# Attention and two MLPs: the second product of the second MLP's first group as seven block products, and stages for x's parts in dead columns of x

## The chip, the cores and the metric

The kernel runs on one core of one Trainium2 chip. The metric is device time in microseconds (us) of one execution, as the median of the runs. TensorE (PE) multiplies, VectorE (DVE) and ScalarE (ACT) work element by element, SyncE (SP) issues the DMAs. Each engine takes its instructions in the order in which they stand in its queue.

## What is computed

A linear attention gives x (2304 tokens, 512 features), and two MLPs follow it. Both have the same shapes; they differ in the function between their two products.

```python
kv = np.einsum('bhsd,bhse->bhde', k, v)
out = np.einsum('bhsd,bhde->bhse', q, kv)
rms = np.sqrt(np.mean(out * out, axis=-1, keepdims=True) + 1e-06)
x = (out / rms * g_norm)            # brought to [2304, 512]
h = x @ w_in                        # [512, 2048], first MLP
x = (np.maximum(h, 0.0) + np.log1p(np.exp(-np.abs(h)))) @ w_out
h = x @ w_in2                       # second MLP
y = np.maximum(0.01 * h, h) @ w_out2
```

All of it is float32. On PE every factor is held as a high part in fp32r and a remainder ("parts"), and each float32 product is three matmuls: high by high, high by low, low by high.

## The kernel before

**Tiling.** The 2304 tokens are cut into NTP = 3 pairs of blocks of BN = 384 tokens. Each MLP's hidden features are cut into NG = 4 groups of 512, so the two MLPs have groups 0 to 3 and 4 to 7. A step t is one group with one token pair, t = 3 * group + pair; there are 24 steps, 0 to 23. Group 4, the second MLP's first group, is steps 12 to 14.

**First product of a step** (`product`, L845). The products of x and the first weight are done as seven block products instead of eight (a scheme of Strassen's kind): 2 stages of 7 products of 6 matmuls with 384 columns, 84 matmuls in a step. The seven combinations of x's blocks ("x's parts") are in `xe`; they are worked out once for each MLP and token pair (`x_part`, with `split_part`), stored to DRAM (`part_store`), and loaded again for each group (`x_load`). In the steps just ahead of the second MLP (t = 11, 12, 13) the parts of the next pair are made from the first MLP's result, which lies in `xy`: four combinations, whose parts go through two stages in `rc` (`xstage`, 6 KiB each), and three plain blocks, split directly into `xe`. A stage can be written again when the store that reads it has landed.

**Second product.** It lags: while step t's first products run, step t - 1's second products run between them. In the groups named in `SG` it is also seven block products (`second`, its `piece`): in the first MLP with 84 matmuls of 384 columns (L1101), in the second with 126 matmuls of 256 columns (L1096) in a step. For that DVE makes differences of the activations (`g_part`, L976), ACT and DVE split seven blocks of them (`parts`, L874 and L879), and both work out seven combinations of the second weight (`w2_part`, L1027 and L1030). Each block's result is added to `xy` by DVE (`to_y`, L1074). In the other groups, 0, 3 and 4, it is the plain product (`quarter`): L1196 in groups 0 and 3, and in group 4 L1214, 72 matmuls of 512 columns in a step, whose results are copied to `xy` (`to_xy`, L729 by DVE or L730 by ACT), since group 4 is the first to write there.

**Buffers.** `xy` holds x and, in place, each MLP's result. `rb` holds the activations' parts and the second weight's (`w2s` of the plain products, `wS` of the block products, in two layouts: one for groups 1 and 2, one for groups 5 to 7). `rc`, `mf` and `lf` hold raw and decoded weights and activations; `cS` is the ring of activation blocks of the block products.

**Order.** All operations are recorded as `op(cost by engine, function, reads, writes)`, and `Plan.run` puts them in order: it walks through a modelled time and takes on each engine, of the operations that are ready, the one due first. The products on PE keep the order in which they are written. The order on DVE, ACT and SP follows from costs and due times.

Of the kernel before, what the change touches and what calls it, by code (L numbers as in the profile page):

```python
# [133 lines left out]
def linear_attention_two_mlps(  # L134
# [209 lines left out]
    def t_d(n, fast=False):  # L344
        return 0.08 + n * (0.8e-3 if fast else 1.04e-3)
# [431 lines left out]
    def x_part(tp, i, stages=(), B=None):  # L777
# [218 lines left out]
    def w2_part(g, i):  # L996


        def blk(a, u):
            at = (3 + 4 * u) * KI // 4  # L1000
            ap = bufs["rc"][:, at:at + 2 * DM].rearrange("p (m f) -> p m f", m=2)
            return ap[:, :, a * 256:(a + 1) * 256]

        def bk(a, u):
            return [k_ for m in range(2) for k_ in fS[u][m].keys(1024 * a, 1024 * (a + 1))]
# [19 lines left out]
        w_ = wS[g // NG][PROD[i][2]]  # L1025
# [25 lines left out]
    def second(t):  # L1051
# [8 lines left out]
        def to_y(i, bank, j0, j1):  # L1060
# [11 lines left out]
            xk = xyk(kcs, c0, n // len(kcs))  # L1072
            op(
                {"D": t_d(n)}, lambda e: nc.vector.tensor_tensor(dst, src, dst, ALU.add),  # L1074
                xk, [("ps", bank)] + xk,
            )

        def piece(i, j):
            w_ = wS[g // NG][PROD[i][2]]
# [224 lines left out]
    for s in range(2 * NT2 + 2):  # L1304
# [17 lines left out]
        for i in range(7):  # L1322
            if t == 0 and i in (0, 3):
                plain(s, i // 3)
            if t < NT2:
# [7 lines left out]
                if t + 1 in fresh and t + 1 > NTP and u == 0:  # L1333
                    x_part((t + 1) % NTP, i, xstage)
# [25 lines left out]
        if g + 1 < 2 * NG:  # L1360
# [14 lines left out]
            if g and not by_pairs and no >= 4:  # L1375
                w2_decode(g + 1, no - 4)
# [36 lines left out]
```

## Time and profile before

| | us |
|---|---|
| median of 3 runs | 800.98 (800.06 to 803.91) |
| the profiled execution | 801.74 |
| its span, first to last instruction | 800.0 |
| PE busy | 787.8 |
| DVE busy | 644.2 |
| ACT busy | 505.9 |

The profiled execution is 0.1% above the median. Busy time is the union of an engine's instructions in the trace, so two that overlap count once; PE is busy without a break from about 85 us to the end. The steps are seen in the trace by their 84 matmuls of L845: step 12 starts at 417.45 us, step 13 at 448.65, step 14 at 480.54, step 15 at 511.92, step 16 at 543.29, step 18 at 602.46. Since the second product lags by a step, group 4's plain second product lies in steps 13 to 15.

### The profile page before, as it was taken

Reading aid. Unit: us, or ns where it says so; the run is one execution under the profiler, and the core shown is the slowest. Engines: PE = TensorE matmul, PEld = TensorE weight load, DVE = VectorE, ACT = ScalarE, POOL = GpSimd, SP = SyncE. Lnnn points to the kernel's source line nnn. Section 1 sums busy time; section 2 is a strip of 40 time slices with the busy share of each in tenths; the row PEclk is TensorE's granted clock in tenths of the full one; section 3 lists DMA queues with packets and bytes.
Section 4 is the critical chain, followed back from the end, with each engine's and each line's share of the span. In section 5 each row is a group of like instructions: output and inputs, shape, how many; then the busy total and the mean of one; then the engine's idle time right before and its main releaser. Section 6 shows DMA issues by size and latency. Waiting matters only on the chain.

```text
span 800.0 us, 12956 instructions
## 1 busy us (share of the span) xinstructions
PE 787.8 (98%) x4962; PEld 774.4 (97%) x4962; DVE 644.2 (81%) x1046; ACT 505.9 (63%) x832; POOL 19.0 (2%) x35
## 2 busy tenths in 40 slices
PE   7899999999999999999999999999999999999997
PEld 6899999999999999999999988989999999999997
DVE  6897996978899987983688866748789997996776
ACT  5788986777666675584476676748457654554341
POOL 3310000000000000000000000000000000000000
PEclk9999999999999999999999999999999999999999
DMA  9990992875864783585776986866745763653814
GB/s 305 320 348 2 344 392 100 325 247 234 319 218 174 291 315 128 217 319 194 289 289 227 401 304 246 313 210 222 275 166 198 295 235 120 252 195 122 315 40 120
DMA packets 77294, 192.48 MB, mean 241 GB/s; under 512 B 11568, under 2 KB 50480, under 8 KB 77232
## 3 DMA queue, kind: packets, MB, share of 16 engines
q1 hardware_dynamic: 75344, 190.73, 66.0%
q10 hardware_dynamic: 1888, 0.92, 0.4%
q8 instruction: 39, 0.64, 0.3%
q14 instruction: 23, 0.19, 0.1%
HBM read 152.31 MB, written 39.32 MB: 240 GB/s over the span
## 4 chain that ended last, share of the span: by engine, by line
PE 95%; DVE 2%; ACT 1%; DMA 1%; SPq 1%; issue 0%; ACTq 0%; DVEq 0%
PE ps L845 42%; PE ps L1096 17%; PE ps L1196 12%; PE ps L1101 11%; PE ps L1214 6%; PE ps L461 2%; PE ps L424 1%; PE ps L939 1%; PE ps L545 1%; DMA mf<-in_moe_w_in_dram 1%; PE ps L416 1%; PE ps L467 0%; SPq L384 0%; PE ps L427 0%; DVE ra L701 0%
## 5 line engine op out<-in xcount | busy, mean ns | idle before, releaser
L845 PE MATMUL ps<-ra 128*128 128x384 f32 x1932 | 387.7, 335 | 0.0
L845 PEld LDWEIGHTS ps<-ra 128*128 128x128 f32 x1932 | 334.9, 188 | 3.8
L874 ACT ACTIVATE rb<-mf 128x768 fp32r<-128x768 f32 x131 | 110.8, 846 | 84.0 <-PE ps L1096 39.2
L1096 PE MATMUL ps<-rb 128*128 128x256 f32 x1134 | 153.1, 281 | 0.0
L1096 PEld LDWEIGHTS ps<-rb 128*128 128x128 f32 x1134 | 148.7, 189 | 0.0
L879 DVE TENSOR_TENSOR rb<-mf,rb 128x768 fp32r<-128x768 f32 x131 | 124.9, 954 | 24.2 <-ACT rb L874 23.5
L1074 DVE TENSOR_TENSOR xy<-ps,xy 128x512 f32<-128x512 f32 (+2 forms) x213 | 116.2, 549 | 30.7 <-PE ps L1096 20.1
L1196 PE MATMUL ps<-rb 128*128 128x384 f32 x576 | 113.7, 334 | 0.0
L1150 DVE TENSOR_TENSOR mf<-ps,mf 128x384 f32<-128x384 f32 x118 | 65.3, 554 | 54.2 <-PE ps L845 53.3
L1196 PEld LDWEIGHTS ps<-rb 128*128 128x128 f32 x576 | 101.1, 188 | 0.0
L1101 PE MATMUL ps<-rb 128*128 128x384 f32 x504 | 100.9, 334 | 0.0
L1143 ACT ACTIVATE mf<-ps 128x384 f32<-128x384 f32 x118 | 57.7, 490 | 58.2 <-PE ps L845 55.1
L1101 PEld LDWEIGHTS ps<-rb 128*128 128x128 f32 x504 | 88.6, 188 | 0.0
L1214 PE MATMUL ps<-rb 128*128 128x512 f32 x216 | 56.8, 394 | 0.0
L1214 PEld LDWEIGHTS ps<-rb 128*128 128x128 f32 x216 | 39.9, 188 | 5.7
L860 ACT ACTIVATE mf<-mf 128x768 f32<-128x768 f32 (+1 forms) x44 | 29.8, 678 | 16.6 <-DVE mf L1150 16.5
L866 ACT ACTIVATE mf<-mf 128x384 f32<-128x384 f32 (+1 forms) x42 | 27.6, 657 | 18.9 <-DVE mf L1150 18.8
L976 DVE TENSOR_TENSOR mf<-mf 128x768 f32<-128x768 f32 x40 | 38.1, 952 | 0.9 <-ACT mf L866 0.3
L1027 ACT ACTIVATE rb<-rc 128x512 fp32r<-128x512 f32 x35 | 21.8, 626 | 6.9 <-PE ps L1214 2.4
L1030 DVE TENSOR_TENSOR rb<-rc,rb 128x512 fp32r<-128x512 f32 x35 | 23.9, 684 | 1.1 <-ACT rb L1027 1.1
L730 ACT ACTIVATE xy<-ps 128x384 f32<-128x384 f32 (+1 forms) x32 | 17.3, 541 | 11.0 <-PE ps L1196 8.9
L461 PE MATMUL ps<-kvm,qt 128*128 128x128 f32 x128 | 18.8, 295 | 2.0 <-DVE xn L523 1.5
(120 smaller groups left out, 791.1 us busy)
## 6 DMA issues: line engine op xcount, KB each, us to landing
ra<-xscr SPq DMA_DIRECT2D x131, 768.0 KB, 6.2
xscr<-ra SPq DMA_DIRECT2D x30, 768.0 KB, 6.9
mf<-in_moe_w_in_dram SPq DMA_DIRECT2D x18, 512.0 KB, 6.6
xscr<-rc SPq DMA_DIRECT2D x12, 768.0 KB, 3.8
mf<-in_moe_w_out_dram SPq DMA_DIRECT2D x17, 512.0 KB, 5.8
lf<-in_moe_w_out_dram SPq DMA_DIRECT2D x15, 512.0 KB, 4.0
lf<-in_moe_w_in_dram SPq DMA_DIRECT2D x14, 512.0 KB, 7.4
qa<-in_q_dram SPq DMA_DIRECT2D x16, 256.0 KB, 5.2
```

The costliest lines, as they stand in the source:

```text
L461: nc.tensor.matmul(ps[4 + i][:, r * P:(r + 1) * P], qt[i][:, at_[r]:at_[r] + P], kvm[i], start=True, stop=True,)
L845: nc.tensor.matmul(o, w_[:, a, c:c + P], e_[:, b, kk, :], start=(not on and kk == 0 and n == 0), stop=(kk == 1 and n == 2), skip_group_che ...
L874: {"A": t_a(n)}, lambda e: nc.scalar.activation(g[:, 0, :, :], c.ap, AF.Copy),
L879: lambda e: nc.vector.tensor_tensor(g[:, 1, :, :], c.ap, g[:, 0, :, :].bitcast(F32), ALU.subtract),
L976: lambda e: nc.vector.tensor_tensor(to.ap, x.ap, y.ap, ALU.subtract),
L1074: {"D": t_d(n)}, lambda e: nc.vector.tensor_tensor(dst, src, dst, ALU.add),
L1096: nc.tensor.matmul(y[:, 256 * (j % 2):256 * (j % 2 + 1)], G_[:, a, m, js], w_[:, b, m, :], **flags)
L1101: nc.tensor.matmul(y[:, :BN], w_[:, a, m, js], G_[:, b, m, :], **flags)
L1143: {"A": t_a(BN)}, lambda e: nc.scalar.activation(c[:, m, :], src, AF.Copy),
L1150: lambda e: nc.vector.tensor_tensor(c[:, m, :], src, c[:, m, :], ALU.add),
L1196: nc.tensor.matmul(y[:, :BN], w_[m][:, a, js], G_[:, b, m, :], start=(u == 0 and m == 0 and i == 0), stop=(u == 1 and m == 1 and i == 2),)
L1214: nc.tensor.matmul(y, G_[:, a, m, js], w_[m][:, b, :], start=(u == 0 and m == 0 and i == 0), stop=(u == 1 and m == 1 and i == 2),)
```

## The change

Group 4 enters `SG`: its second product becomes seven block products of 256 columns, as in groups 5 to 7. What that needs is moved:

- `wS` has one layout for all groups.
- Group 4's second weight is decoded into `half` (in `lf` and `mf`) in the last two stages of group 3, and `w2_part` takes it from there, with `sqr` for its temporary block.
- The results of the first four blocks that meet a column of `xy` are copied (by DVE or ACT), those of the other three added.
- The temporaries of x's combinations for pairs 1 and 2 are in `rc` (`xt_late`), where the stages were; the stages for these two pairs are columns of `xy` (`Dead`): those of the pair before, whose x parts have all been taken and whose second result isn't written yet. Such a stage is four rows of 384 elements in a partition instead of one run of 1536.

```diff
+    xt_late = [Reg("rc", at * KI, [2, BN]) for at in (3, 6)]
+
+    class Dead:
+        def __init__(self, c):
+            self.c = c
+        def __getitem__(self, i):
+            return xy[:, :, self.c:self.c + BN].bitcast(F32R).rearrange(
+                "p (a b) n -> p a b n", a=2
+            )[i]
...
-    SG = (1, 2, NG + 1, NG + 2, NG + 3)
+    SG = (1, 2, NG, NG + 1, NG + 2, NG + 3)
...
-    wS = [
-        {j: Reg("rb", at * KI, [2, 2, 256]) for j, at in zip((1, 4, 5, 6, 3, 2, 0), ats)}
-        for ats in ((46, 50, 30, 34, 38, 42, 26), (38, 42, 46, 50, 30, 34, 26))
-    ]
+    wS = {
+        j: Reg("rb", at * KI, [2, 2, 256])
+        for j, at in zip((1, 4, 5, 6, 3, 2, 0), (46, 50, 30, 34, 38, 42, 26))
+    }
...
+        x_ = xt_late if stages and tp else xt
...
     def part_store(tp, i, e_):
+        def fn(e):
+            if isinstance(e_, Dead):
+                nc.sync.dma_start(
+                    out=xscr[7 * tp + i].rearrange("p (k n) -> p k n", k=KC),
+                    in_=xy[:, :, e_.c:e_.c + BN],
+                )
+            else:
+                nc.sync.dma_start(out=xscr[7 * tp + i], in_=flat(e_).ap.bitcast(F32))
...
     def w2_part(g, i):
+        f_ = half[::-1] if g == NG else fS
...
-        r.append((lambda: fT.ap, fT.keys()))
+        r.append(
+            (lambda: sqr.bitcast(F32).rearrange("p (m f) -> p m f", m=2), [("sqr", 0), ("sqr", 1)])
+            if g == NG else (lambda: fT.ap, fT.keys())
+        )
...
-            op(
-                {"D": t_d(n)}, lambda e: nc.vector.tensor_tensor(dst, src, dst, ALU.add),
-                xk, [("ps", bank)] + xk,
-            )
+            to_xy(dst, src, n, g == NG and i in (0, 1, 2, 6), bank, xyk(kcs, c0, n // len(kcs)))
...
-                    x_part((t + 1) % NTP, i, xstage)
+                    tp = (t + 1) % NTP
+                    x_part(tp, i, [Dead((2 * tp - 2 + j) * BN) for j in range(2)] if tp else xstage)
...
-            if g and not by_pairs and no >= 4:
+            if g == NG - 1 and no >= 4:
+                decode_pair(F + 2 * (no - 4), 1, 5 - no)
+            elif g and not by_pairs and no >= 4:
                 w2_decode(g + 1, no - 4)
```

On PE, where step 13 begins, the rows of before are these (`ps_83` to `ps_86` take first products, `ps_87` to `ps_90` second ones; L1196 is the end of group 3):

```order
L845 MATMUL ps_83<-ra 128x384 x6
L1196 MATMUL ps_90<-rb 128x384 x3
L1214 MATMUL ps_87<-rb 128x512 x3
L845 MATMUL ps_85<-ra 128x384 x6
L1214 MATMUL ps_88<-rb 128x512 x3
L1214 MATMUL ps_89<-rb 128x512 x3
L845 MATMUL ps_83<-ra 128x384 x6
L1214 MATMUL ps_87<-rb 128x512 x3
```

and the same place of the changed kernel, where L870 is the first product, L1222 group 3's second and L1122 the second product in blocks:

```order
L870 MATMUL ps_83<-ra 128x384 x6
L1222 MATMUL ps_90<-rb 128x384 x3
L1122 MATMUL ps_87<-rb 128x256 x6
L870 MATMUL ps_85<-ra 128x384 x6
L1122 MATMUL ps_87<-rb 128x256 x6
L870 MATMUL ps_83<-ra 128x384 x6
L1122 MATMUL ps_88<-rb 128x256 x6
L1122 MATMUL ps_89<-rb 128x256 x6
```

The plain rows of three matmuls with 512 columns are replaced by rows of six with 256; up to here PE's queue is unchanged.

On DVE at the same place, before (L735 takes group 3's last results, L793 and L758 make x's parts, L637, L617 decode a weight, L1150 takes first products):

```order
L735 TENSOR_TENSOR xy<-ps_90,xy 128x384
L758 TENSOR_TENSOR rc<-mf,rc 128x768
L793 TENSOR_TENSOR mf<-xy,mf 128x768
L793 TENSOR_TENSOR mf<-xy 128x768
L758 TENSOR_TENSOR rc<-mf,rc 128x768
L637 SCALAR_TENSOR_TENSOR lf<-lf,sqr 128x512
L617 TENSOR_SCALAR sqr<-mf 128x512
L1150 TENSOR_TENSOR mf<-ps_85,mf 128x384
```

and in the changed kernel (L753 adds results, L747 copies them, L813 and L776 make x's parts, L904 and L1001 the activations', L1060 the second weight's, L1176 takes first products):

```order
L753 TENSOR_TENSOR xy<-ps_90,xy 128x384
L813 TENSOR_TENSOR rc<-xy 128x768
L904 TENSOR_TENSOR rb<-mf,rb 128x768
L1060 TENSOR_TENSOR rb<-lf,rb 128x512
L747 COPY xy<-ps_87 128x2x2x128
L776 TENSOR_TENSOR xy<-rc,xy 128x2x384
L813 TENSOR_TENSOR rc<-xy,rc 128x768
L1060 TENSOR_TENSOR rb<-mf,rb 128x512
L904 TENSOR_TENSOR rb<-rc,rb 128x768
L1176 TENSOR_TENSOR mf<-ps_85,mf 128x384
L1060 TENSOR_TENSOR rb<-mf,rb 128x512
L1176 TENSOR_TENSOR mf<-ps_83,mf 128x384
```

Between the first of these rows and the first that takes a first product there were six rows, and now there are eight; weight decoding has moved behind them. In the changed kernel 33 rows stand from the first row above, which waits for PE's last L1222, to the row `L1176 TENSOR_TENSOR rc<-ps_84,rc 128x384`, for which PE waits: 17 with 768 elements, 7 with 512, 6 with 384, 3 with 256. Between those two points PE has 114 matmuls of 256 columns and 72 of 384.

On SP at about the same place, before:

```order
L583 DMA mf<-in_moe_w_in_dram 128x4x256
L828 DMA ra<-xscr 128x1536
L814 DMA xscr<-ra 128x1536
L583 DMA lf<-in_moe_w_in_dram 128x4x256
L814 DMA xscr<-rc 128x1536 x2
L588 DMA mf<-in_moe_w_out_dram 128x1024
L588 DMA lf<-in_moe_w_out_dram 128x1024
L814 DMA xscr<-rc 128x1536
```

and in the changed kernel (L834 is the store from columns of x, L839 the other store, L853 the load, L601 a raw weight):

```order
L601 DMA mf<-in_moe_w_in_dram 128x4x256
L834 DMA xscr<-xy 512x1x384 x3
L853 DMA ra<-xscr 128x1536
L601 DMA lf<-in_moe_w_in_dram 128x4x256
L839 DMA xscr<-ra 128x1536
L853 DMA ra<-xscr 128x1536
L834 DMA xscr<-xy 512x1x384
L853 DMA ra<-xscr 128x1536
```

Stores from `rc` have become stores from `xy` in 512 runs of 384 elements instead of 128 of 1536, eight in all, and the second weight's loads follow later.

## Rows read from the trace of the kernel before

**Rows 1.** The page: busy us, share, instructions; then the chain that ended last.
```profile
PE 787.8 (98%) x4962; PEld 774.4 (97%) x4962; DVE 644.2 (81%) x1046; ACT 505.9 (63%) x832; POOL 19.0 (2%) x35
...
PE 95%; DVE 2%; ACT 1%; DMA 1%; SPq 1%; issue 0%; ACTq 0%; DVEq 0%
```
**Rows 2.** Waits of PE from 100 to 800 us: the heading, no row follows.
```profile
engine line waited for: us in total, times, longest us
```
**Rows 3.** Windows by step (11 to 16, 18): busy us and counts, clock, DMA.
```profile
386.25:417.45 31.20, 31.20 (x181) 31.20 (x181) 24.38 (x37) 19.73 (x30) 0.00 (x0) 1.00 0.73 275
417.45:448.65 31.20, 31.20 (x181) 31.20 (x181) 25.56 (x39) 21.73 (x33) 0.00 (x0) 1.00 0.75 289
448.65:480.54 31.89, 31.89 (x160) 28.71 (x160) 22.93 (x33) 22.96 (x37) 0.00 (x0) 1.00 0.90 341
480.54:511.92 31.38, 31.38 (x158) 28.19 (x157) 19.61 (x31) 22.14 (x38) 0.00 (x0) 1.00 0.76 281
511.92:543.29 31.37, 31.37 (x158) 28.19 (x156) 19.07 (x29) 18.11 (x30) 0.00 (x0) 1.00 0.67 241
543.29:572.87 29.58, 29.58 (x211) 29.58 (x210) 25.06 (x39) 19.81 (x32) 0.00 (x0) 1.00 0.72 251
...
602.46:632.05 29.59, 29.59 (x213) 29.59 (x212) 28.51 (x47) 19.51 (x31) 0.00 (x0) 1.00 0.65 236
```
**Rows 4.** Windows of L1096 alone in step 16: matmuls, weight loads.
```profile
543.29:572.87 29.58, 17.07 (x126) 16.70 (x126) 1.00 0.72 251
```
**Rows 5.** Timeline of PE in step 15: start us, us, instructions.
```profile
521.35 1.55 PE L1214 MATMUL ps<-rb 128*128 128x512 f32 x6
522.74 1.21 PE L845 MATMUL ps<-ra 128*128 128x384 f32 x6
```
**Rows 6.** Timeline of PE in step 17.
```profile
576.38 1.21 PE L845 MATMUL ps<-ra 128*128 128x384 f32 x6
577.43 1.59 PE L1096 MATMUL ps<-rb 128*128 128x256 f32 x12
578.85 1.21 PE L845 MATMUL ps<-ra 128*128 128x384 f32 x6
```
**Rows 7.** Timeline of DVE in step 18, rows that follow back to back.
```profile
603.00 0.95 DVE L879 TENSOR_TENSOR rb<-mf,rb 128x768 fp32r<-128x768 f32 x1
603.87 0.95 DVE L701 TENSOR_TENSOR ra<-mf,ra 128x768 fp32r<-128x768 f32 x1
...
607.92 0.42 DVE L1074 TENSOR_TENSOR xy<-ps,xy 128x256 f32<-128x256 f32 x1
608.26 0.68 DVE L637 SCALAR_TENSOR_TENSOR lf<-lf,sqr 128x512 int32<-128x512 int32 x1
608.86 0.95 DVE L879 TENSOR_TENSOR rb<-mf,rb 128x768 fp32r<-128x768 f32 x1
609.73 0.55 DVE L1150 TENSOR_TENSOR rc<-ps,rc 128x384 f32<-128x384 f32 x1
610.20 1.21 DVE L701 TENSOR_TENSOR ra<-mf,ra 128x1024 fp32r<-128x1024 f32 x1
```
**Rows 8.** The page's DMA issues: count, KB each, median us to landing.
```profile
ra<-xscr SPq DMA_DIRECT2D x131, 768.0 KB, 6.2
...
xscr<-rc SPq DMA_DIRECT2D x12, 768.0 KB, 3.8
```
**Rows 9.** Line L814, the stores of x's parts: all its landings.
```profile
DMA to landing us min/median/max: 3.2/6.5/10.0
```
**Rows 10.** Line L773, the stores of plain blocks from x, 256 runs each.
```profile
DMA to landing us min/median/max: 4.2/5.7/6.6
```
**Rows 11.** Waits of ACT from 380 to 560 us: in total, times, longest.
```profile
ACT rc L763 <- DMA xscr<-rc: 1.5, 1, 1.5
```
**Rows 12.** Timeline of ACT in step 12: a copy of a first product.
```profile
434.29 0.49 ACT L1143 ACTIVATE mf<-ps 128x384 f32<-128x384 f32 x1 [0.71 <-PE ps L845]
```
**Rows 13.** The page's groups: a weight load beside matmuls of 256 columns (busy, mean ns).
```profile
L1096 PEld LDWEIGHTS ps<-rb 128*128 128x128 f32 x1134 | 148.7, 189 | 0.0
```

More of the change, by code (lines that the diff above doesn't have):

```diff
@@ L286, in linear_attention_two_mlps, with keys @@
     xstage = [Reg("rc", at * KI, [2, 2, BN], F32R) for at in (0, 6)]
+    xt_late = [Reg("rc", at * KI, [2, BN]) for at in (3, 6)]
[6 more added lines that the diff above has]
+            )[i]
+        def keys(self, lo=0, hi=None):
+            row = 4 * BN
+            hi = 4 * row if hi is None else hi
+            return xyk(range(lo // row, (hi - 1) // row + 1), self.c, BN)
     xb = {(j, k_): Reg("rc", (6 * j + 3 * k_) * KI, [2, BN]) for j in range(2) for k_ in range(2)}
@@ L786, in x_part @@
             return
+        x_ = xt_late if stages and tp else xt
         def T_(t):
-            return (lambda: xt[t].ap), xt[t].keys()
+            return (lambda: x_[t].ap), x_[t].keys()
         def minus(t, a, b):
             def fn(e):
-                ENG[e].tensor_tensor(xt[t].ap, a[0](), b[0](), ALU.subtract)
-            op({"D": t_d(2 * BN)}, fn, a[1] + b[1], xt[t].keys())
+                ENG[e].tensor_tensor(x_[t].ap, a[0](), b[0](), ALU.subtract)
+            op({"D": t_d(2 * BN)}, fn, a[1] + b[1], x_[t].keys())
             return T_(t)
@@ L811, in part_store @@
     def part_store(tp, i, e_):
-        op(
-            {"S": 2.25},
-            lambda e: nc.sync.dma_start(out=xscr[7 * tp + i], in_=flat(e_).ap.bitcast(F32)),
-            e_.keys(), [("xs", tp, i)],
-        )
+        def fn(e):
[6 more added lines that the diff above has]
+                nc.sync.dma_start(out=xscr[7 * tp + i], in_=flat(e_).ap.bitcast(F32))
+        op({"S": 2.25}, fn, e_.keys(), [("xs", tp, i)])
     def flat(e_):
@@ L996, in w2_part @@
     def w2_part(g, i):
+        f_ = half[::-1] if g == NG else fS
         def blk(a, u):
-            at = (3 + 4 * u) * KI // 4
-            ap = bufs["rc"][:, at:at + 2 * DM].rearrange("p (m f) -> p m f", m=2)
-            return ap[:, :, a * 256:(a + 1) * 256]
+            f0 = f_[u][0]
+            ap = bufs[f0.name][:, f0.at // 4:f0.at // 4 + 2 * DM]
+            return ap.rearrange("p (m f) -> p m f", m=2)[:, :, a * 256:(a + 1) * 256]
         def bk(a, u):
-            return [k_ for m in range(2) for k_ in fS[u][m].keys(1024 * a, 1024 * (a + 1))]
+            return [k_ for m in range(2) for k_ in f_[u][m].keys(1024 * a, 1024 * (a + 1))]
         r = [(lambda a=a, u=u: blk(a, u), bk(a, u)) for a in range(2) for u in range(2)]
-        r.append((lambda: fT.ap, fT.keys()))
+        r.append(
+            (lambda: sqr.bitcast(F32).rearrange("p (m f) -> p m f", m=2), [("sqr", 0), ("sqr", 1)])
+            if g == NG else (lambda: fT.ap, fT.keys())
+        )
         def combine(to, x, y, sign):
@@ L1024, in w2_part @@
         src, sk = r[(2, 4, 2, 4, 0, 3, 1)[i]]
-        w_ = wS[g // NG][PROD[i][2]]
+        w_ = wS[PROD[i][2]]
         hk, lk = w_.keys(0, 2048), w_.keys(2048)
@@ L1071, in to_y @@
                 dst, src = xy[:, kcs[0], c0:c0 + BN], ps[bank][:, :BN]
[L1072 to L1076 removed]
+            to_xy(dst, src, n, g == NG and i in (0, 1, 2, 6), bank, xyk(kcs, c0, n // len(kcs)))
         def piece(i, j):
[L1079 removed]
+            w_ = wS[PROD[i][2]]
             G_ = g_reg((t, "S", i))
```

## The prediction

> **What bounds the kernel now.** I read the page first. PE is busy for 787.8 of 800.0 us, and the chain that ended last is 95% PE [rows 1]; busy alone could hide stalls, so I asked for PE's waits: from 100 us to the end there is none [rows 2]. PE's queue therefore sets the time, and a change is worth what it takes out of that queue, less what PE then has to wait. Next come the windows by step [rows 3]: steps 14 and 15, with the plain second product of group 4, take 31.38 and 31.37 us, and steps 16 and 18, with the block form, 29.58 and 29.59. Step 13 takes 31.89, because three matmuls of group 3 run over into it. The granted clock is 1.00 in all of them, the upper of the two levels. DVE is the engine to watch: 28.51 us busy in step 18, where PE still waits for nothing, but only 19 to 26 in steps 12 to 15.
>
> **PE's part of the change.** In steps 13 to 15 the 72 matmuls of 512 columns become the 126 of 256 columns that a later step has [rows 4]. First way: step by step. A step with 84 first matmuls and 72 plain ones is 31.37 us, one with 84 and 126 block ones is 29.58 to 29.59; the difference is 1.78 us, and three steps give 5.34 us. Second way, from the timeline: six of 512 columns start at 521.35 and the next row at 522.74, 1.39 us or 0.232 each [rows 5]; twelve of 256 take from 577.43 to 578.85, 1.42 us or 0.118 each [rows 6]. 72 x 0.232 - 126 x 0.118 is 16.7 - 14.9 = 1.8 us, the same. So PE's queue gets 5.3 us shorter. The order shows the replacement and nothing else on PE.
>
> A rule speaks against this. The rows first: with 256 columns a step has 126 weight loads instead of 72 [rows 4], each 189 ns long [rows 13], and still a matmul follows every 118 ns [rows 6], so loads run beside matmuls. The Trainium skill, "TensorE: Matmul & The Clock Gate", section "The mechanism", says that a weight load overlaps running matmuls only when it goes to other row groups, while all loads here take all 128 rows; by that, more and smaller matmuls would expose more loads. The same section also allows a background weight buffer, and by rows 6 that is the case that holds. What the rule would cost is the third rival below.
>
> **DVE's part.** The second product in blocks needs, over three steps: 9 more splits of activations (21 instead of 12) and 12 differences, all of 768 elements; for the weight 4 combinations and 7 splits in place of 4 old ones, of 512; 9 additions of 512 and 9 of 256, where copies stood; and copies, of which the new order gives DVE 2 of 512 and 4 of 256 in place of 3 of 512. Back to back a 768 costs 0.87 us (603.00 to 603.87), a 512 0.60 (608.26 to 608.86), a 256 0.34 (607.92 to 608.26), a 384 0.47 (609.73 to 610.20) [rows 7]; the 0.95 shown as duration overlaps the next. Sum: 21 x 0.87 + 7 x 0.60 + 9 x 0.94 + 0.8 = 18.3 + 4.2 + 8.5 + 0.8 = 31.7 us. Is there room? DVE is busy 25.56 + 22.93 + 19.61 + 19.07 = 87.2 of 125.8 us in steps 12 to 15 [rows 3], so 38.7 are free; PE's gain takes 5.3 of them, 33.3 stay. The added work fits with 1.6 us to spare if none of it lies outside these steps; step 11 (6.8 us idle) and step 16 (4.5) give some air.
>
> So tight a fit must be looked at by place. In the new order the longest crowded stretch of DVE's queue is the one at the start of step 13: 33 rows from the one that waits for PE's last L1222 to the one that PE waits for: 17 x 0.87 + 7 x 0.60 + 6 x 0.47 + 3 x 0.34 = 22.8 us. PE meanwhile has 114 x 0.118 + 72 x 0.174 (six of 384 from 576.38 to 577.43, 1.05 us [rows 6]) = 26.0 us. Some 3 us are spare there, before waits of DVE for ACT or DMA. I take DVE's part as hidden, cost 0, and keep 2.6 us as its other end (first rival).
>
> **ACT, weights and stores.** ACT gets 12 more instructions (9 splits of 768, 3 of 512); at no more than 0.95 us each that is under 12 us, against 40.9 us idle in steps 12 to 15 (125.8 less 21.73 + 22.96 + 22.14 + 18.11 [rows 3]): hidden. The second weight's decoding is the same work; half of it is recorded in step 11 instead of step 9, at most 2 x 3 x 0.60 = 3.6 us of DVE against 6.8 idle there: hidden. Its loads move back on SP's queue, past loads and stores of x's parts; a load of x's parts is used half a step, some 15 us, after it is issued and lands in 6.2 us [rows 8], so SP may be held up to 8 us before PE waits: cost 0, and beyond that cover, PE waits for every us. One layout of `wS` puts group 5's weights where group 4's blocks lie, as between groups 5, 6 and 7 before, where PE never waited [rows 2]: cost 0.
>
> The eight stores from columns of x carry the same bytes in 512 runs instead of 128. No row shows such a store. Nearest: the stores from `rc`, 3.8 us to landing [rows 8], all stores of x's parts 3.2 to 10.0 [rows 9], and stores with 256 runs of the same length and half the bytes, 4.2 to 6.6 [rows 10]. Doubling the last gives an estimate of 8.4 to 13.2 as the upper end; the lower is 3.2, a little faster than now. I take the 6.5 of rows 9, since that is the middle of what DMAs of this size do in these steps. Who waits for a landing: the third and fourth split of a pair, because a stage is written again (ACT, then DVE, with all queued behind them); ACT waited so once, 1.5 us [rows 11], and PE not at all. The loads behind these stores on SP have the same cover of 8 us.
>
> **The sum.** Against the profiled execution: 801.74 - 5.34 + 0 = 796.4. The median lies 0.76 us below that execution, so I expect a median of 795.7.
>
> **The rivals.**
> *DVE becomes the bound.* For: 87.2 + 31.7 = 118.9 us of DVE in 120.5 us is 98.7% full over four steps; the fullest step that the trace shows is 28.51 of 29.59, 96.4% [rows 3]. If DVE can't be fuller than that, four steps hold 116.2 us and 2.6 us come back as waits of PE for accumulators that DVE has not yet emptied: 798.3. Against: the spare 3 us of the stretch, and the idle time in steps 11 and 16.
> *Stores in short runs hold ACT.* Place: ACT's queue in steps 12 and 13, at the splits into a stage that is still being read; behind them stand the copies of first products (0.49 us [rows 12]) whose accumulators PE needs again about 2.5 us later (the next product starts 2.47 us on [rows 6]), so that some 2 us of delay cost nothing. With a landing of L us instead of 6.5, two spells (one for each pair) cost PE 2 x (L - 6.5 - 2) us. At 8.5 us it begins, from 11.2 the whole gain is gone, and at 13.2, the upper estimate, 9.4 us are lost: 805.1, slower than before. Against: DMA's share in these steps is 0.75 and 0.90 [rows 3], not full, and stores that took up to 10.0 us [rows 9] never reached PE [rows 2]. The Trainium skill, "Perfetto Trace Analysis", section "DMA Optimizations", calls DMAs of under 2 KB costly for each transfer; a run here is 1.5 KB, and the rows bear out at most the estimate of 8.4 to 13.2.
> *Weight loads show.* If the 162 additional loads (3 x 54) ran unhidden for their 189 ns [rows 13], 30.6 us would be added: 826.3. Rows 6 rule this out but for a surprise.
>
> **How the numbers follow.** Forecast, all of PE's gain but at most 1.2 us: 0.76. DVE becomes the bound: 0.17. Stores hold ACT: 0.06, half of it past the point of 11.2 us. Weight loads show: 0.01. The range: the fastest run of before, 800.06, less 5.34 is 794.7, and a store that lands sooner changes nothing on PE; I take 794.4. At the top it reaches the first rival, 798.3, with 0.3 for spread: 798.6. What lies above is the second and third rival and a part of the first. A measurement of this kernel can tell about 0.5% from no change, that is 4.0 us: under 797.0 counts as faster. The forecast falls there except for an edge of 0.06, so faster is 0.70; the edge, the first rival and most of the second make same 0.27; slower, over 805.0, is 0.03: the second rival's end and the third.
>
> **What the profile after would show.** Right: no rows of 512 columns on PE; steps 13 to 15 at 30.1, 29.6 and 29.6 us; PE's waits after 100 us still none; DVE near 28 to 29 us in steps 12 to 15; stores from x landing in under 8 us. DVE the bound: waits of PE for DVE at L1176 or L753 in steps 13 to 16, some 2.6 us in all. Stores: waits of ACT at L781 for the DMA `xscr<-xy`, and PE waits for ACT at L1169. Wrong altogether would be a clock under 1.00, or time lost outside steps 11 to 16.

## The result, and the profile after

The changed kernel takes 795.74 us (median of 5 runs, 794.87 to 796.28); the kernel before, run beside it, 801.98 us (median of 5, 800.06 to 804.88). The ratio is 0.9917, with a 95% interval from 0.9891 to 0.9944: 0.8% faster. The prediction was 795.7 us, with a range from 794.4 to 798.6.

The profiled execution of after took 796.14 us, with a span of 794.4. Its page, against [rows 1], first the busy time of the engines (busy us, share of the span, number of instructions), then the chain that ended last:

```profile
PE 782.5 (99%) x5124; PEld 778.2 (98%) x5124; DVE 675.0 (85%) x1094; ACT 514.2 (65%) x848; POOL 19.0 (2%) x35
...
PE 93%; DVE 3%; ACT 1%; DMA 1%; SPq 1%; issue 0%; ACTq 0%; DVEq 0%
```

PE does 162 matmuls more than before (5124 against 4962) in 5.3 us less. DVE has 30.8 us more to do and ACT 8.3 us more. The waits of PE from 100 us on, as in [rows 2], are still a heading with no row under it:

```profile
engine line waited for: us in total, times, longest us
```

So the cover held: all that DVE, ACT and the DMAs got lies beside PE's work. The timeline of PE in step 14 (start us, us, instructions) shows the new pattern, where [rows 5] had six matmuls of 512 columns:

```profile
486.53 1.21 PE L870 MATMUL ps<-ra 128*128 128x384 f32 x6
487.58 1.59 PE L1122 MATMUL ps<-rb 128*128 128x256 f32 x12
489.00 1.21 PE L870 MATMUL ps<-ra 128*128 128x384 f32 x6
```

Twelve of 256 columns take 1.42 us from start to start, as in [rows 6]. The windows of steps 11 to 18, to be held against [rows 3]; after the length come the busy us (and count) of PE, PEld, DVE, ACT and POOL, then clock, DMA share and GB/s:

```profile
386.30:417.50 31.20, 31.20 (x182) 31.20 (x182) 25.41 (x39) 20.14 (x31) 0.00 (x0) 1.00 0.75 280
417.50:448.70 31.20, 31.20 (x182) 31.20 (x182) 30.59 (x46) 23.43 (x36) 0.00 (x0) 1.00 0.88 319
448.70:478.80 30.10, 30.10 (x215) 30.10 (x215) 29.77 (x44) 24.73 (x41) 0.00 (x0) 1.00 0.84 299
478.80:508.38 29.58, 29.58 (x212) 29.58 (x211) 25.02 (x39) 22.90 (x40) 0.00 (x0) 1.00 0.82 314
508.38:537.97 29.59, 29.59 (x213) 29.59 (x211) 28.56 (x46) 22.98 (x39) 0.00 (x0) 1.00 0.69 247
537.97:567.55 29.58, 29.58 (x212) 29.58 (x211) 27.34 (x45) 21.00 (x35) 0.00 (x0) 1.00 0.70 253
567.55:597.14 29.59, 29.59 (x212) 29.59 (x211) 26.51 (x43) 17.04 (x26) 0.00 (x0) 1.00 0.68 250
597.14:626.73 29.59, 29.59 (x213) 29.59 (x211) 28.61 (x47) 19.51 (x31) 0.00 (x0) 1.00 0.65 236
```

Steps 13, 14 and 15 lost 1.79, 1.80 and 1.78 us; steps 11, 12, 16 and 18 last as before. DVE is busy for 30.59 of 31.20 and 29.77 of 30.10 us in steps 12 and 13, 98 and 99%, and PE doesn't wait. The eight stores from the dead columns of x landed after this time (least, median, most):

```profile
DMA to landing us min/median/max: 3.7/5.5/9.9
```

That is no slower than the stores of x's parts before [rows 9], although they go in shorter runs. Held against the eight stores from `rc` that they replace, in the same steps of the kernel before, it is the same: those landed after 5.6 us in the median (the 3.8 of [rows 8] is for all twelve), and in e1 below, where the stages alone are moved, the median is 6.2.

### The profile page after: what moved, and what is told of

Its sections match the earlier page's. It is cut to its first block, busy times and chain, and to the rows that moved or that the text cites. A ratio compares the mean times of both kernels' runs of the same rounds, so it can differ in the third digit from the quotient of the medians.

```text
span 794.4 us, 13352 instructions
## 1 busy us (share of the span) xinstructions
PE 782.5 (99%) x5124; PEld 778.2 (98%) x5124; DVE 675.0 (85%) x1094; ACT 514.2 (65%) x848; POOL 19.0 (2%) x35
## 4 chain that ended last, share of the span: by engine, by line
PE 93%; DVE 3%; ACT 1%; DMA 1%; SPq 1%; issue 0%; ACTq 0%; DVEq 0%
PE ps L870 42%; PE ps L1122 23%; PE ps L1222 13%; PE ps L1127 11%; PE ps L479 1%; PE ps L964 1%; DMA mf<-in_moe_w_in_dram 1%; PE ps L442 1%; PE ps L563 1%; DVE ra L719 1%; DVE mf L698 0%; DVE ss L504 0%; SPq L402 0%; PE ps L434 0%; DVE xn L541 0%
## 5 line engine op out<-in xcount | busy, mean ns | idle before, releaser
L870 PE MATMUL ps<-ra 128*128 128x384 f32 x1932 | 387.4, 335 | 0.0
L870 PEld LDWEIGHTS ps<-ra 128*128 128x128 f32 x1932 | 332.0, 188 | 0.0
L1122 PE MATMUL ps<-rb 128*128 128x256 f32 x1512 | 204.8, 281 | 0.0
L1122 PEld LDWEIGHTS ps<-rb 128*128 128x128 f32 x1512 | 198.8, 189 | 0.0
L899 ACT ACTIVATE rb<-mf 128x768 fp32r<-128x768 f32 x138 | 116.6, 845 | 87.7 <-PE ps L1122 44.6
L753 DVE TENSOR_TENSOR xy<-ps,xy 128x512 f32<-128x512 f32 (+2 forms) x255 | 139.4, 550 | 31.8 <-PE ps L1122 18.1
L904 DVE TENSOR_TENSOR rb<-mf,rb 128x768 fp32r<-128x768 f32 x138 | 131.6, 953 | 17.3 <-ACT rb L899 16.3
L1222 PE MATMUL ps<-rb 128*128 128x384 f32 x576 | 113.6, 334 | 0.0
L1222 PEld LDWEIGHTS ps<-rb 128*128 128x128 f32 x576 | 101.1, 188 | 0.0
L1176 DVE TENSOR_TENSOR mf<-ps,mf 128x384 f32<-128x384 f32 x114 | 63.0, 553 | 38.1 <-PE ps L870 37.0
L1127 PEld LDWEIGHTS ps<-rb 128*128 128x128 f32 x504 | 88.6, 188 | 0.0
L1001 DVE TENSOR_TENSOR mf<-mf 128x768 f32<-128x768 f32 x48 | 45.7, 952 | 0.8
L748 ACT ACTIVATE xy<-ps 128x384 f32<-128x384 f32 (+2 forms) x35 | 17.4, 496 | 13.2 <-PE ps L1222 9.2
L1060 DVE TENSOR_TENSOR rb<-rc,rb 128x512 fp32r<-128x512 f32 x35 | 23.8, 684 | 0.9 <-ACT rb L1057 0.9
L641 ACT ACTIVATE sqr<-mf 128x512 uint16<-128x512 uint16 x28 | 21.7, 776 | 0.0
L1169 ACT ACTIVATE rc<-ps 128x384 f32<-128x384 f32 x24 | 11.7, 489 | 12.8 <-PE ps L870 12.4
```

The lines of the kernel that those rows point to most:

```text
L870: nc.tensor.matmul(o, w_[:, a, c:c + P], e_[:, b, kk, :], start=(not on and kk == 0 and n == 0), stop=(kk == 1 and n == 2), skip_group_che ...
L899: {"A": t_a(n)}, lambda e: nc.scalar.activation(g[:, 0, :, :], c.ap, AF.Copy),
L904: lambda e: nc.vector.tensor_tensor(g[:, 1, :, :], c.ap, g[:, 0, :, :].bitcast(F32), ALU.subtract),
L1001: lambda e: nc.vector.tensor_tensor(to.ap, x.ap, y.ap, ALU.subtract),
L1122: nc.tensor.matmul(y[:, 256 * (j % 2):256 * (j % 2 + 1)], G_[:, a, m, js], w_[:, b, m, :], **flags)
L1127: nc.tensor.matmul(y[:, :BN], w_[:, a, m, js], G_[:, b, m, :], **flags)
```

## The experiments

Every ratio is to the kernel before, run beside the others. "Step" is a step as in the windows above. Where nothing else is said, PE waits for nothing after 100 us.

| run | edit | ratio to before, 95% | steps 12 to 15, us |
|---|---|---|---|
| after | the change | 0.9917 [0.9891, 0.9944] | 31.20, 30.10, 29.58, 29.59 |
| e1 | before, stages alone | 0.998 [0.9961, 0.9998] | 31.20, 31.89, 31.37, 31.38 |
| e2 | before, matmuls halved | 1.0016 [0.9997, 1.0035] | 31.20, 32.26, 31.74, 31.75 |
| e3 | after + 6 sums + tile | 1.0018 [1.0002, 1.0034] | 31.65, 30.10, 29.54, 29.54 |
| e4 | after + 21 sums + tile | 1.0029 [1.0012, 1.0047] | 31.65, 30.10, 29.55, 29.55 |
| e5 | after + tile of 8 bytes | 1.0052 [1.0032, 1.0072] | 31.65, 30.10, 29.54, 29.54 |
| e6 | after + 21 sums | 0.9934 [0.9917, 0.9951] | 31.20, 30.09, 29.59, 29.60 |
| e7 | after + 42 sums | 1.0106 [1.009, 1.0122] | 31.20, 35.74, 32.70, 33.57 |
| e8 | after, one more group by blocks | 1.0007 [0.9992, 1.0021] | 32.49, 38.66, 29.60, 29.59 |
| e9 | after, stores twice | 0.996 [0.9945, 0.9975] | 31.20, 30.11, 30.51, 30.63 |
| e10 | after + tile of 64 bytes | 1.012 [1.01, 1.0139] | 31.76, 30.54, 30.05, 30.05 |
| e11 | e8, one pair without stages | 0.9941 [0.9927, 0.9955] | 30.48, 34.82, 30.43, 29.59 |
| e12 | after without dead stages | 0.9929 [0.9915, 0.9942] | 31.20, 30.10, 29.58, 29.59 |

**e1, one part alone: the stages.** The kernel before with the new stages and their stores, and the plain second product as it was.

```diff
...
-                    x_part((t + 1) % NTP, i, xstage)
+                    tp = (t + 1) % NTP
+                    x_part(tp, i, [Dead((2 * tp - 2 + j) * BN) for j in range(2)] if tp else xstage)
```

> The kernel before with only the stages moved: x's parts of pairs 1 and 2 go through dead columns of x, with their temporaries in rc; group 4 keeps its plain second product. Theory (the gain is PE's shorter queue, the stages cost and give nothing): ratio to before 1.000, within 0.2%; steps 13 to 15 stay at 31.9, 31.4 and 31.4 us, no wait of PE after 100 us. Rival (the stores in 512 short runs hold ACT): ACT waits at its split for the DMA xscr<-xy, by several us, and PE waits behind it, 1 to 9 us. Rival (the stages bring part of the gain): up to 5 us faster.

The steps last as in the kernel before. Its span, 797.4 us, was 2.6 us under that of before, but its step 1 begins 2.1 us earlier already (84.13 against 86.21), where both programs are still the same, and its last matmul starts earlier by the same 2.1 us (792.96 against 795.03); the rest of the 2.6 lies behind the last matmul. So no step gained by the stages, and the difference is above all one of the first stretch (below, under what was not expected). The ratio is not quite 1: its interval ends at 0.9998, and the median is 1.0 us lower. The steps show nothing of that.

**e2, more and smaller matmuls alone.** Each matmul of 512 columns of the kernel before is cut into two of 256, so that the weights are loaded twice; nothing else is done.

```diff
-                    nc.tensor.matmul(
-                        y, G_[:, a, m, js], w_[m][:, b, :],
...
+                    for h in range(2):
+                        nc.tensor.matmul(
+                            y[:, 256 * h:256 * (h + 1)], G_[:, a, m, js],
+                            w_[m][:, b, 256 * h:256 * (h + 1)],
...
```

> The kernel before with each matmul of 512 columns of group 4's second product cut into two of 256 columns with the same weight loaded again: same work, twice as many matmuls and weight loads, 144 in a step. Theory (a weight load hides behind a matmul of 256 columns): 144 x 0.118 - 72 x 0.232 = 0.3 us a step, 1.0 us in three steps slower, 0.1%. Rival (weight loads show): 72 more loads of 0.189 us in each of three steps, 41 us slower, 5%.

Windows of steps 13 to 15:

```profile
446.43:478.69 32.26, 32.26 (x233) 32.26 (x233) 22.92 (x33) 22.99 (x38) 0.00 (x0) 1.00 0.90 342
478.69:510.43 31.74, 31.74 (x230) 31.74 (x229) 19.61 (x31) 21.95 (x38) 0.00 (x0) 1.00 0.76 280
510.43:542.18 31.75, 31.75 (x231) 31.75 (x229) 19.04 (x29) 18.16 (x30) 0.00 (x0) 1.00 0.64 236
```

72 additional matmuls with as many additional loads cost 0.37 us in a step, 5 ns each: 144 x 0.118 is 17.0 us where 72 x 0.232 was 16.7. A load of 189 ns [rows 13] that showed would have cost 13.6 us in each step. The loads are hidden, and the gain comes from the smaller number of columns that the block form streams (126 x 256 instead of 72 x 512).

**e3 and e4, more work for DVE.** The changed kernel with 6 and with 21 additional sums of 768 elements on DVE in the three steps of group 4, into a new tile of 8 bytes.

```diff
+    spare = const.tile([P, 2], F32, name="spare")
...
+        if g == NG and i in range(7):      # e3: i in (2, 5)
+            op(
+                {"D": t_d(2 * BN)},
+                lambda e: nc.vector.tensor_reduce(spare, src.ap, axis=AX, op=ALU.add),
+                src.keys(), [("spare",)], due=plan.pe + 5.0,
+            )
```

> The changed kernel with two more DVE instructions (a sum over 768 elements, some 0.87 us each) in each of group 4's three steps, six in all, 5.2 us of DVE, due like the work beside them; nothing else reads them. DVE is busy 30.6 of 31.2, 29.8 of 30.1, 25.0 of 29.6 and 28.6 of 29.6 us in steps 12 to 15 of the changed kernel, 6.5 us free. Theory (DVE is hidden, with little to spare): 0 to 1 us slower than the changed kernel, time to before 0.992 to 0.994. Rival (DVE already sets the time there): all 5.2 us come out, ratio to before 0.999.

> As the run before it, with seven such instructions in each of the three steps: 21, 18.3 us of DVE. The free time of steps 12 to 15, 6.5 us, and of steps 16 and 17, some 5 us, can't hold it. Theory: DVE becomes the bound in steps 12 to 16, and PE waits 4 to 12 us: ratio to before 0.997 to 1.008. If PE does not wait at all, DVE's share of the time says nothing here, and work that is due later gives way.

The median rose by 7 to 8 us, but not where the sums stand: PE has no wait, and steps 13 to 17 are as short as in after. What got longer were steps far from the sums. This is step 5 of e3, in the first MLP; in after it lasts 29.12 us:

```profile
213.82:243.36 29.54, 29.54 (x169) 29.54 (x169) 25.52 (x41) 17.72 (x28) 0.00 (x0) 1.00 0.64 233
```

The sums were not to blame, so both runs say nothing of them by their time. The new tile was suspected: with it, `rb` begins at byte 151840 of a partition instead of 151808, while `ra`, `mf`, `rc` and `lf` stay.

**e5 and e10, the tile alone.** Nothing but the tile and one memset of it, with 8 bytes (so `rb` moves by 32) and with 64 (so `rb` moves by 64).

```diff
+    spare = const.tile([P, 2], F32, name="spare")      # e10: [P, 16]
+    nc.vector.memset(spare, 0.0)
```

> The changed kernel with nothing added but a tile of 8 bytes per partition, set once at the start; it is given the place at which the tile of the packed B operands stood, and that tile begins 32 bytes later. Theory (the address of the operands set the time lost in e3 and e4, not the sums): the matmuls of 384 columns are each about 5 ns slower, a step of the first MLP by blocks takes 29.54 us instead of 29.12, a plain step 31.65 instead of 31.20, PE waits for nothing after 100 us, the span is about 801 us and the ratio to the kernel before 1.000 to 1.003. Rival (the additional sums cost the time): one small instruction at the start changes nothing, the steps last as in the changed kernel and the ratio is 0.992.

> As e5, but the added tile is 64 bytes per partition, so that the tile of the packed B operands begins 64 bytes later than in the changed kernel instead of 32. Theory (what counts is where the tile stands within 64 bytes): as in the changed kernel, steps of the first MLP by blocks 29.12 us, plain steps 31.20 us, ratio to the kernel before 0.992. Rival (any move of the tile costs, or the additional tile and its memset): 29.54 and 31.65 us as in e5, ratio 1.003 to 1.007.

Steps 5 and 14 of e5, then of e10:

```profile
213.91:243.44 29.53, 29.53 (x169) 29.53 (x169) 25.50 (x41) 17.70 (x28) 0.00 (x0) 1.00 0.64 231
486.12:515.66 29.54, 29.54 (x212) 29.54 (x211) 25.03 (x39) 22.92 (x40) 0.00 (x0) 1.00 0.83 317
```

```profile
215.02:244.70 29.68, 29.68 (x169) 29.68 (x169) 25.54 (x41) 17.72 (x28) 0.00 (x0) 1.00 0.63 228
488.70:518.76 30.06, 30.06 (x213) 30.06 (x211) 25.05 (x39) 23.06 (x40) 0.00 (x0) 1.00 0.80 304
```

e5 confirms that the tile costs all that e3 and e4 had lost: the steps of the three are the same to 0.01 or 0.02 us, so that the 21 sums of e4, held against e5, cost no step anything. e10 refutes my reading that the place within 64 bytes counts: a move by 64 costs more than one by 32, 0.56 us in step 5 and 0.48 in step 14. The memset can't be it, since e3 and e4 have the tile without it and the same steps. What it is stays open (below).

**e6 and e7, more work for DVE without a new tile.** The sums go into `graw`, a tile that is there already: one for each block product of group 4 (21), then two (42).

```diff
+        for _ in range(1 if g == NG else 0):      # e7: 2
+            op(
+                {"D": t_d(2 * BN)},
+                lambda e: nc.vector.tensor_reduce(
+                    graw, src.ap.rearrange("p a n -> p (a n)"), axis=AX, op=ALU.add
+                ),
+                src.keys(), [("graw", 0)], due=plan.pe + 5.0,
+            )
```

> The changed kernel with one additional VectorE sum of 768 elements for each block product of the three steps of the second MLP's first group, into a tile that exists already, so that no tile moves: 21 sums, some 18 us at 0.87 us each. Theory: VectorE has some 6.5 us free in steps 12 to 15 and some 6 in steps 16 and 17, and what doesn't fit is put off past step 17; PE waits little or not at all, ratio to the kernel before 0.991 to 0.995. Rival (VectorE becomes the bound): what exceeds the free time is waited for by PE, so 18 minus 6.5 is up to 11.5 us more, ratio 0.996 to 1.006, with waits of PE on VectorE in steps 13 to 17.

> As e6, with two additional sums for each block product: 42 sums, some 36.6 us. Theory: this is past what steps 12 to 17 have free (some 12.5 us), VectorE falls behind by more than the buffers between it and PE cover, and PE waits: 5 to 24 us more than the changed kernel, ratio to the kernel before 0.998 to 1.022. Rival (VectorE's work can be put off to the end of the second MLP without limit): PE doesn't wait and the ratio stays at 0.992.

e6, steps 13 to 15:

```profile
448.99:479.08 30.09, 30.09 (x214) 30.09 (x214) 29.85 (x42) 23.41 (x40) 0.00 (x0) 1.00 0.65 234
479.08:508.67 29.59, 29.59 (x212) 29.59 (x211) 29.22 (x44) 22.73 (x40) 0.00 (x0) 1.00 0.99 360
508.67:538.27 29.60, 29.60 (x212) 29.60 (x211) 28.96 (x45) 23.84 (x42) 0.00 (x0) 1.00 0.64 229
```

Eighteen us more on DVE cost nothing. Only part of that shows in DVE's busy time, 683.0 us against 675.0: ACT has 860 instructions against 848 and DVE 1103 against 1094, so the planner, which knows of the sums, gave about a dozen of DVE's to ACT. What DVE itself did more is thus 8.0 us. With 42 the cover is gone. e7, steps 13 to 15, and PE's waits (in total, times, longest):

```profile
447.04:482.78 35.74, 31.95 (x215) 31.54 (x214) 35.71 (x50) 23.95 (x40) 0.00 (x0) 0.95 0.59 216
482.78:515.48 32.70, 30.27 (x206) 28.99 (x205) 32.70 (x46) 22.70 (x39) 0.00 (x0) 1.00 0.87 318
515.48:549.05 33.57, 30.64 (x206) 28.98 (x205) 33.51 (x51) 25.63 (x43) 0.00 (x0) 1.00 0.55 190
```

```profile
PE ps L1130 <- DVE xy L753: 5.5, 4, 2.4
PE ps L870 <- ACT ra L715: 0.9, 1, 0.9
PE ps L870 <- DVE mf L1184: 0.8, 1, 0.8
PE ps L1130 <- DVE rb L904: 0.8, 1, 0.8
```

DVE is busy for 101.92 of 102.01 us. This is what "DVE is the bound" looks like: the length of a step is DVE's busy time, and PE waits above all for accumulators that DVE empties at L753, the place that the prediction's first rival had named. It came somewhere between 21 and 42 sums, that is 18 and 37 us of them; since the planner gave 12 and 13 instructions to ACT, DVE's own busy time had risen by 8.0 us in e6 and by 24.2 in e7 (683.0 and 699.2 against 675.0).

**e8, the same exchange for one group more.** Group 3, the last of the first MLP, by blocks too; since its blocks then take the place of `xstage`, the parts of x of the first pair are made straight into `xe` in step 11.

```diff
-    SG = (1, 2, NG, NG + 1, NG + 2, NG + 3)
+    SG = (1, 2, NG - 1, NG, NG + 1, NG + 2, NG + 3)
...
+                elif t + 1 == NG * NTP and u == 1:
+                    x_part(0, i, late=True)
```

> The changed kernel with the group before it (the last of the first MLP, steps 10 to 12) by block products too, and the parts of x of its first pair made in step 11's second stage. Theory: the same exchange again, three steps from 31.20 to 29.12 us as in the first MLP's other groups by blocks, 6.2 us in all, so a span near 788 us and a ratio to the kernel before of 0.984. Rival (VectorE becomes the bound): steps 11 to 13 hold the sums of this group, the parts of x and the first results of the next group together; VectorE was 98 to 99 per cent busy in steps 12 and 13 already, so what comes on top is waited for, and of the 6.2 us up to all goes, ratio 0.988 to 1.000, with waits of PE on VectorE in steps 11 to 14.

Windows of steps 11 to 13, PE's first two waits, and PE's timeline in step 13:

```profile
383.26:412.38 29.12, 29.12 (x170) 29.12 (x170) 26.26 (x41) 19.04 (x28) 0.00 (x0) 1.00 0.39 146
412.38:444.87 32.49, 30.56 (x170) 28.90 (x169) 31.84 (x49) 24.46 (x38) 0.00 (x0) 1.00 0.65 232
444.87:483.53 38.66, 33.39 (x212) 32.05 (x211) 33.18 (x48) 25.15 (x42) 0.00 (x0) 0.91 0.72 244
```

```profile
PE ps L870 <- DMA ra<-xscr: 4.7, 3, 3.4
PE ps L1127 <- DVE xy L753: 1.0, 1, 1.0
```

```profile
465.08 2.26 PE L870 MATMUL ps<-ra 128*128 128x384 f32 x6 [3.42 <-DMA ra<-xscr]
467.14 1.48 PE L1122 MATMUL ps<-rb 128*128 128x256 f32 x6
```

Steps 10 and 11 gained as the theory said (29.12 each), and steps 12 and 13 lost more than that: steps 10 to 14 last 159.0 us in all and 152.8 in after, so that the gain of group 4 is gone as well. VectorE's load was part of it, as the rival said, but step 13 has 5.5 us in which DVE is idle: there PE waited 3.42 us for a part of x that had been made late, stored and loaded again. The wait costs twice. The granted clock of the step is 0.91, and right behind the wait six matmuls of 384 columns take 2.06 us (465.08 to 467.14) where 1.05 is usual, and the next six, of 256, take 1.28 (to 468.42) where 0.71 is: they ran at the lower of the two levels, 1.2 GHz instead of 2.4.

**e9, the stores twice.** Each store from the dead columns is issued a second time, to a spare place.

```diff
+        def again(e):
+            nc.sync.dma_start(
+                out=xscr[7 * NTP + 1 + 7 * tp + i].rearrange("p (k n) -> p k n", k=KC),
+                in_=xy[:, :, e_.c:e_.c + BN],
+            )
...
+        if isinstance(e_, Dead):
+            op({"S": 2.25}, again, e_.keys(), [("xs2", tp, i)])
```

> The changed kernel with each of the eight stores from the dead columns of x issued twice, the second time to a spare place in device memory. Theory (the stores cost nothing, since nobody waits for their landing): the later pieces land perhaps 2 to 4 us later, PE waits for nothing after 100 us, steps 13 to 15 last 30.1, 29.6 and 29.6 us, ratio to the kernel before 0.990 to 0.994. Rival (stores in short runs hold ScalarE): each store's landing takes up to twice as long, so some 11 us or more, ScalarE waits for xscr from xy, and PE waits up to 10 us, ratio 0.996 to 1.004.

Windows of steps 14 and 15, then the landing of the first of each two stores:

```profile
482.18:512.69 30.51, 30.06 (x212) 29.42 (x211) 22.19 (x38) 17.64 (x32) 0.00 (x0) 1.00 1.01 403
512.69:543.32 30.63, 30.27 (x211) 29.67 (x211) 30.36 (x48) 25.70 (x43) 0.00 (x0) 1.00 0.60 205
```

```profile
DMA to landing us min/median/max: 6.0/8.0/11.2
```

My "cost nothing" was too strong: steps 14 and 15 are 2.0 us longer. But the rival's way is not the one: ScalarE has no wait for `xscr` from `xy`. With twice the stores the DMA engines are full through step 14 (share 1.01 against 0.82), and the second weight's loads go out later on SP's queue. After first, where step 14 begins at 478.80 us, then e9, where it begins at 482.18:

```profile
482.72 0.33 SPq L606 DMA_DIRECT2D lf<-in_moe_w_out_dram  x1
488.59 0.33 SPq L606 DMA_DIRECT2D mf<-in_moe_w_out_dram  x1
```

```profile
488.16 0.33 SPq L606 DMA_DIRECT2D lf<-in_moe_w_out_dram  x1
495.06 0.32 SPq L861 DMA_DIRECT2D ra<-xscr  x1
495.49 0.37 SPq L606 DMA_DIRECT2D mf<-in_moe_w_out_dram  x1
```

Counted from the start of the step, the first goes out at 6.0 us instead of 3.9, the second at 13.3 instead of 9.8. The second is not held by the stores alone: the planner, which counts the additional stores, put a load of x's part ahead of it on SP's queue, and that load waited 6.5 us for PE to be done with its place. DVE's order differs in step 14 as well. DVE is then busy for only 22.19 us in step 14 and has 30.36 to do in step 15, where PE waits 0.6 us in sum and runs with gaps. So e9 changes the order besides the stores, and whether the 2.0 us come from the full DMA engines or from the order stays open.

**e11, e8 without the way through device memory for the second pair.** Its parts are made half a step later, straight into `xe`.

```diff
-                if t + 1 in fresh and t + 1 > NTP and u == 0:
...
-                elif t + 1 == NG * NTP and u == 1:
-                    x_part(0, i, late=True)
+                if t + 1 == NG * NTP + 2 and u == 0:
+                    x_part(2, i, [Dead((2 + j) * BN) for j in range(2)], late=True)
+                elif t + 1 in fresh[NTP:NTP + 2] and u == 1:
+                    x_part((t + 1) % NTP, i, late=True)
```

> As e8, but the parts of x of the second pair are made half a step later and straight into their operand's place, so that they are neither stored nor loaded again before the first product reads them; the third pair's are still made in the dead columns. Theory (in e8 the sums put the parts of x late, and PE then waited for their way through device memory): the 4.7 us of PE's waits on loaded parts go, and with them most of the time at the lower clock, step 13 falls from 38.7 to some 31 to 34 us, ratio to the kernel before 0.990 to 0.996. Rival (VectorE's load alone is the bound in steps 12 and 13): it holds the same sums, steps 12 and 13 together stay near 70 us, ratio 0.999 to 1.002.

Windows of steps 12 to 14:

```profile
411.44:441.92 30.48, 29.67 (x169) 29.02 (x169) 29.52 (x48) 21.93 (x34) 0.00 (x0) 1.00 0.47 173
441.92:476.74 34.82, 31.64 (x211) 29.61 (x211) 34.82 (x50) 27.50 (x45) 0.00 (x0) 1.00 0.61 232
476.74:507.17 30.43, 29.90 (x213) 29.69 (x211) 26.41 (x41) 23.17 (x41) 0.00 (x0) 1.00 1.02 407
```

Steps 12 and 13 fall from 71.2 to 65.3 us, PE's waits on loaded parts from 4.7 to 0.5 us, and the clock stays at 1.00: most of the 5.9 us were that wait and what it did to the clock. It is not an exact price, since the other waits changed too. What is left is DVE, 34.82 busy of 34.82 us in step 13. Steps 10 to 14 last 154.0 us in all (159.0 in e8), those of after 152.8: the further group gains 6.2 us and costs 7.4. It doesn't beat the change.

**e12, the other part undone: the stages.** The changed kernel, with the parts of the second and third pair made in the step's second stage straight into `xe`.

```diff
...
-                    x_part(tp, i, [Dead((2 * tp - 2 + j) * BN) for j in range(2)] if tp else xstage)
+                if t + 1 == NG * NTP and u == 0:
+                    x_part(0, i, xstage)
+                elif t + 1 in fresh[NTP + 1:] and u == 1:
+                    x_part((t + 1) % NTP, i, (), late=True)
```

> The changed kernel without the stages in the dead columns: the parts of x of the second and third pair are made half a step later, in the step's second stage, straight into their operand's place (the exchange of the second product for seven block products stays). They are then stored, but not loaded again before the first product reads them. Theory A (the stages are needed): the seven operands of a step are made in the same 15 us in which the place of each comes free, VectorE's work bunches in the second halves of steps 12 and 13 where it is 98 to 99 per cent busy, and PE waits for x's low parts at the start of steps 13 and 14: 1 to 5 us more than the changed kernel, ratio to the kernel before 0.993 to 0.998. Theory B (what counts is the sum of VectorE's work, which is the same, and the loads fall away): no wait of PE, ratio 0.990 to 0.993.

Windows of steps 12 to 14:

```profile
417.83:449.03 31.20, 31.20 (x182) 31.20 (x182) 29.27 (x45) 22.07 (x33) 0.00 (x0) 1.00 0.62 244
449.03:479.13 30.10, 30.10 (x215) 30.10 (x215) 28.84 (x43) 25.03 (x41) 0.00 (x0) 1.00 0.53 200
479.13:508.71 29.58, 29.58 (x212) 29.58 (x211) 28.24 (x44) 24.27 (x40) 0.00 (x0) 1.00 0.73 281
```

Theory B holds: the steps are those of after to 0.01 us, with a lower share of DMA (0.62, 0.53 and 0.73 against 0.88, 0.84 and 0.82) and DVE's work spread more evenly. The whole gain comes from the block products. The dead columns give the stages a place, but the kernel is as fast without them.

## Why the prediction was right, point by point

- **PE's term, 5.34 us.** Steps 13 to 15 are 5.37 us shorter by the windows, and the last matmul starts 5.3 us earlier (789.7 against 795.0). Both ways of working it out from [rows 3 to 6] held, because PE never waited before and doesn't now. e1 and e12 show that no other part of the change moves a step.
- **Weight loads hidden.** Shown by e2, where they were doubled alone: 0.37 us in a step. The rule cited against the change, the Trainium skill, "TensorE: Matmul & The Clock Gate", section "The mechanism", in its narrow reading (a load overlaps matmuls only when it goes to other row groups) doesn't describe these matmuls. The background weight buffer, which the same section allows, agrees with the 0.37 us and with [rows 6]; that the loads go there no run shows.
- **DVE's 31.7 us hidden.** The size was right: the page has 30.8. The place was off: 118.9 us had been forecast for steps 12 to 15, and 113.9 are there; steps 11, 16 and 17 took 1.0, 2.3 and 2.9 us more. So DVE is full in steps 12 and 13 (98 and 99%) and has 4.6 us free in step 14. The forecast of "28 to 29 us" for each of the four was wrong for three of them. ACT got 16 instructions more (848 against 832), not 12, and 8.3 us, within the 12 us allowed for it.
- **The first rival's premise**, that DVE may not be fuller than 96.4% of a step, was drawn from the fullest step that the trace happened to show. It falls: 99% without a wait in after, and 100% in e11's step 13, there with PE waiting. Nor did its load come: 113.9 us lie in the four steps, less than the 116.2 that it would have let through. It was given 0.17. By e6, 21 x 0.87 = 18 us of further sums cost nothing; by e7, 42 x 0.87 = 37 us make steps 13 to 16 longer by 14.2 us. The margin is larger than the 1.6 us of the sum, since work can go to later steps and the planner hands some of it to ACT; in DVE's own busy time it is at least 8.0 us and less than 24.2.
- **The stores.** Taken at 6.5 us to landing, measured 5.5; the upper estimate of 8.4 to 13.2, from doubled bytes, was too pessimistic as a median (the slowest took 9.9). ACT waits for none of them. e9 shows that twice the stores are nonetheless not free: at a median of 8.0 us, 2.0 us are lost, and not by ACT's waits for a landing. The second weight's loads go out 2.1 and 3.5 us later in the step there, which the prediction's cover ("SP may be held up to 8 us", for the loads of x's parts) didn't look at; how much of the 2.0 us is theirs is not shown.
- **Median against profiled execution.** The 0.76 us that I took off came from one execution of before; the span shows 5.6 us of difference, 5.4 of them in steps 13 to 15. That the median came out at 795.74 against 795.7 is luck to the tenth: I had started from a median of before of 800.98, and beside the change it was 801.98, from which 5.34 leads to 796.6. The medians differ by 6.2 us, of which the steps explain 5.4; the medians of before in the five comparisons lie between 800.77 and 801.98.

## What to carry to other kernels

When an engine's queue is gapless over the whole stretch, as PE's was here, an exchange of its instructions is worth the difference of their queue times (5.34 us worked out, 5.37 measured), and one step of the same kernel that has the new form already is the best price list. Ask of the covering engines not only how much is free but how far work can be put off before somebody waits: here DVE could be 98 to 99% full for 61 us. And add no tile, however small, without looking at what it moves and at the steps that shouldn't change.

## What was not expected of the hardware

**Moving a tile changes the speed of the matmuls.** With `rb` 32 bytes further on, the matmuls of 384 columns follow each other within a row of the order on average after 175.6 ns instead of 173.3 (operands in `rb`) and 173.8 (operands in `ra`, which didn't move); with 64 bytes after 177.0 to 177.8. Those of 256 columns go from 118.9 to 118.3 and 119.2. In after the gaps of a step of the first MLP are 173 or 174 throughout; in e5 three of 185 ns come at the same places of every 24 matmuls, in e10 two in every 12. From the start of step 1 to the last matmul after takes 703.5 us, e5 708.2 and e10 715.2: in the steps a tile of 8 bytes costs 4.7 us and one of 64 bytes 11.8. The ratios, 1.0052 and 1.012 instead of 0.9917, say 1.4 and 2.0%, but they hold the first stretch too, which varies by itself (below); e3 and e4, with the same 8 bytes, have 1.0018 and 1.0029. Since the matmuls that read `ra` alone slow down too, it isn't the address of a matmul's own operands alone; whether it is the pattern of two neighbouring matmuls' reads or the writes of other engines into `rb`, no run tells.

**The clock falls after a short wait.** In e8 a wait of 3.42 us behind some shorter ones was followed by matmuls of twice the length. In e7 the longest wait was 2.4 us, and the granted clock of that step is 0.95; in e11, where none is over 1.1 us, it is 1.00. In after, without waits, the granted clock is 1.00 in every step.

**The first stretch makes the spread.** Up to the first block product of step 1, where the programs are the same, e11 took 83.83 us and e9 89.62 (0 to that product; columns as in the windows above):

```profile
0.00:83.83 83.83, 77.36 (x594) 74.15 (x595) 69.46 (x154) 65.89 (x137) 19.57 (x35) 1.00 0.79 250
```

```profile
0.00:89.62 89.62, 81.37 (x594) 78.19 (x595) 70.54 (x154) 65.98 (x137) 20.00 (x35) 0.94 0.76 234
```

After that the steps that no edit touches repeat to 0.01 or 0.02 us. A difference of a few us between single executions of this kernel must therefore be looked for there first, and step lengths tell more than spans.
